# Whole expert matrices in one load each, a second pair of early input weights, first output tiles of 128 tokens, and a new order

## The chip, the cores and the metric

The kernel runs on one core of one Trainium2 chip. The metric is the time of one execution on the device in microseconds. The kernel before takes 282.68 us, the median of 3 runs (282.34 to 283.34).

## The reference

Three stages follow one another. An attention layer with 2 batches, 8 heads, 768 tokens and 64 numbers per head looks at a window of 15 tokens to each side and at 24 pooled keys. A soft mixture of 8 experts with 4 slots each sends all 1536 tokens (512 numbers each) through `phi`. A softplus layer of 2048 hidden units ends it.

```python
k_sum = k.reshape(B, H, nb, 32, D).max(axis=3); v_sum = v.reshape(B, H, nb, 32, D).mean(axis=3)
mask_l = np.abs(pos[:, None] - pos[None, :]) < 16
scores_s = scale * np.einsum('bhsd,bhnd->bhsn', q, k_sum) + np.log(32)
...                                   # softmax over [local, pooled], times [v, v_sum] -> x
logits = x @ phi
d = softmax(logits, axis=0); slot_input = (d.T @ x).reshape(8, 4, 512)
for e in range(8):
    slot_out[e] = np.maximum(slot_input[e] @ w1[e], 0.0) @ w2[e]
x = softmax(logits, axis=1) @ slot_out.reshape(32, 512)
h = x @ w_in
return (np.maximum(h, 0.0) + np.log1p(np.exp(-np.abs(h)))) @ w_out
```

The softmaxes are written out in the reference with their maximum and sum. Weights: `w1` is 8 x 512 x 1024, `w2` 8 x 1024 x 512, `w_in` 512 x 2048, `w_out` 2048 x 512, all float32 in the result. The kernel reads `w_in` and `w_out` as 64-bit numbers and cuts float32 values out of their bits.

## The kernel before, in words

Everything that the kernel issues is a task with a name and one to three numbers. Two tables, `ORDER_A` (attention, routing, loads of most expert weights) and `ORDER_B` (experts and output stage), list the tasks, and `run` calls them in that order. Each engine has its own instruction stream and takes its instructions in that order, one after the other; a suffix such as `:DVE` picks the engine of a copy. All loads and stores are issued by SP, also in that order, and SP waits when the next load's buffer isn't free. `warm n` puts n filler matmuls of 480 columns into PE's stream; their result is not used.

*Loads.* Large buffers of 128 x 4096 float32 (`slots`, s0 to s9) are used in turn for the heads' q, k and v, then for the expert matrices. Each `w1` matrix (512 rows of 4 KB, 2 MB) and each `w2` matrix (2 MB) comes in two halves of 1 MB, tasks `w1 e n` and `w2 e h`. `wi c h` loads 256 columns of the input weights (1 MB), `wo c h` 256 rows of the output weights (1 MB); the first of each come in halves of 0.5 MB (`wi 0 0 0` and `wi 0 0 1`, `wo 0 0 0` and `wo 0 0 1`).

*Conversion.* The raw 64-bit weights become float32 by one scaling on ACT (`wia`, `woa`; L720) and three integer operations on DVE (`wib c 0` to `wib c 2`, `wob`; lines L726, L728 and L731), where c now counts the loads of 256. Output weights are also split into a high part `wh` (ACT) and a low part `wl` (DVE, L779).

*Attention and routing.* Per 128 tokens and head group: scores `sc`, maximum `mx`, subtraction `sub`, exponential `ex`, transposes `tr` with copies `tc`, the product `av` and a division `dv`. Then logits (`xt`, `xc`, `lt`, `lc`, `lm`, `ln`), the softmax over tokens, and the slot inputs `siT`. Three filler matmuls stand before the second transpose of the maximum (`warm 3`).

*Experts.* For pairs of experts E, `hu E n` multiplies the slot inputs with half of each of two `w1` matrices (L801, 16 matmuls of 512 columns each), `hr` is the relu, `ht` and `hc` turn the hidden units, and `dn e h` multiplies them with half a `w2` matrix (4 matmuls), all summed in one PSUM bank. Twelve filler matmuls stand among these. The last half, expert 7's second, is apart: `so` (ACT) copies the sum, `yl` multiplies, `ya` (DVE) adds, `yt` (PE) turns it, and `ye` copies it to `soT`. `ct` and `cc` turn the combine weights.

*Output stage.* It doesn't form x: the experts' sum is first multiplied with the input weights. For the first 128 columns this is `swc 0 j` (PE, 8 matmuls), `swd` (ACT or DVE copy of the high part) and `swe` (DVE subtraction, low part), later `qa` to `qe` for four blocks at a time. The result, `SW`, is one operand of `ha n`, the hidden units of one block J of 128 hidden units for 768 tokens (two matmuls of 384 columns, L966). `hx` (ACT softplus, L974), `hh` (ACT, high part) and `hl` (DVE, low part, L779) follow, and `m n t p` adds the products with the output weights to one of six PSUM tiles of 128 tokens (L996). There are 32 visits n: J = 0 and 1 for the first 768 tokens, then J = 0 to 15 for the second 768, then J = 2 to 15 for the first; `leave` parks or adds the sums and `out` stores them. `f` has one PSUM buffer of two banks, `e` two buffers, `gh` and `gl` three each.

## Time and profile before

| | |
|---|---|
| median of 3 runs | 282.68 us (282.34 to 283.34) |
| profiled execution | 281.86 us, its span 280.1 us |
| busy: PE, PEld | 268.9 us (96%), 190.1 us (68%) |
| busy: DVE, ACT, POOL | 158.7 us (57%), 143.3 us (51%), 35.6 us (13%) |
| read from memory, written | 60.15 MB, 3.15 MB |

The engines are PE (matmul), PEld (its weight loads, which overlap it), DVE (vector), ACT (activation), POOL and SP (which issues the DMAs). Times are microseconds from the start of the span, durations of one instruction nanoseconds. A row of a table by stage has the stretch, its length, then the busy time and the number of instructions of PE, PEld, DVE, ACT and POOL, the granted clock of PE (1.00 is full), the share of the 16 DMA engines that was busy, and GB/s. A row of the chain of waits or of a timeline has the start, the duration and the instruction, out<-in by the program's names. A row of instructions by line has the count, the busy time and the mean of one in ns, then the idle time of the engine just before them and what ended it. A row of DMAs has their count, the KB of each and the us from issue to landing.

### The profile page before, as it was taken

How to read it: one execution, taken by the hardware profiler on the slowest of the kernel's cores; microseconds unless marked ns; L12 is line 12 of the kernel's file. 1: busy time of each engine (PE TensorE's matmuls, PEld its weight loads, DVE VectorE, ACT ScalarE, POOL GpSimd, SP SyncE). 2: the span in 40 equal slices, each digit the busy share in tenths (PEclk: the TensorE clock that was granted, in tenths of full speed). 3: DMA queues.
4: the chain of work that ended last, by engine and by line, in shares of the span. 5: the costliest groups of instructions: out<-in, count | busy, mean ns of one | idle time of the engine just before them, and what ended most of it. 6: DMA issues, size and time to landing. Idle time of an engine off the chain costs nothing.

```text
span 280.1 us, 5571 instructions
## 1 busy us (share of the span) xinstructions
PE 268.9 (96%) x2335; PEld 190.1 (68%) x2335; DVE 158.7 (57%) x244; ACT 143.3 (51%) x216; POOL 35.6 (13%) x91
## 2 busy tenths in 40 slices
...
GB/s 258 405 396 383 415 413 401 419 416 418 415 414 375 420 410 416 407 397 398 397 251 400 8 0 0 2 0 0 2 0 114 111 2 0 0 0 2 0 74 151
DMA packets 17064, 63.65 MB, mean 227 GB/s; under 512 B 1936, under 2 KB 2320, under 8 KB 12944
## 3 DMA queue, kind: packets, MB, share of 16 engines
...
q8 instruction: 18, 0.29, 0.4%
q14 instruction: 6, 0.05, 0.0%
HBM read 60.15 MB, written 3.15 MB: 226 GB/s over the span
## 4 chain that ended last, share of the span: by engine, by line
PE 72%; DVE 12%; ACT 6%; issue 4%; DMA 3%; SPq 1%; POOL 1%; DVEq 0%; ACTq 0%; POOLq 0%
PE acc L996 36%; PE h_ps L801 5%; PE so_ps L823 5%; PE av L365 4%; PE tpa L349 4%; PE f_ps L966 3%; DMA s<-in_k 3%; PE sc L327 2%; DVE gl L779 2%; DVE wo L728 2%; DVE wo L731 2%; ACT AB L167 2%; PE tpx L387 2%; DVE wf L728 1%; DVE whl L779 1%
## 5 line engine op out<-in xcount | busy, mean ns | idle before, releaser
L996 PE MATMUL acc<-whl,gh 128*128 128x512 f32 (+1 forms) x386 | 104.3, 392 | 0.0
L996 PEld LDWEIGHTS acc<-whl,gh 128*128 128x128 f32 x386 | 71.4, 188 | 14.3 <-issue 0.8
L779 DVE TENSOR_TENSOR gl<-e,gh 128x768 fp32r<-128x768 f32 (+1 forms) x33 | 30.3, 931 | 52.8 <-PE acc L996 26.3
L996 PE MATMUL acc<-whl,gl 128*128 128x512 f32 (+1 forms) x193 | 57.7, 393 | 0.3 <-DVE gl L779 0.3
L974 ACT ACTIVATE e<-f_ps 128x768 f32<-128x768 f32 (+1 forms) x33 | 26.0, 792 | 40.3 <-PE f_ps L966 25.0
L996 PEld LDWEIGHTS acc<-whl,gl 128*128 128x128 f32 x193 | 36.0, 188 | 9.3 <-DVE gl L779 2.0
L167 ACT ACTIVATE gh<-e 128x768 fp32r<-128x768 f32 (+1 forms) x33 | 26.7, 823 | 13.2 <-PE acc L996 12.9
L167 ACT ACTIVATE s<-s 64x520 f32<-64x520 f32 (+4 forms) x20 | 14.1, 719 | 8.3 <-DMA s<-in_v 8.0
L966 PE MATMUL f_ps<-cs 128*128 128x384 f32 x64 | 16.7, 343 | 1.1 <-ACT e L974 1.0
L365 PE MATMUL av<-s,AB 120*64 120x65 f32 x384 | 15.7, 226 | 1.0 <-ACT AB L167 0.4
L365 PEld LDWEIGHTS av<-s,AB 120*64 120x64 f32 x384 | 13.0, 137 | 5.0 <-issue 3.6
L332 DVE TENSOR_REDUCE m<-sc 128x8 f32<-128x960 f32 x12 | 13.8, 1149 | 4.2 <-PE sc L327 4.2
L167 ACT ACTIVATE AB<-tpa 120x512 f32<-120x512 f32 x23 | 13.5, 595 | 5.3 <-PE tpa L349 5.0
L259 POOL COPY s<-vs 24x520 f32<-24x520 f32 x24 | 14.2, 622 | 12.2 <-ACT vs L167 11.7
L349 PE MATMUL tpa<-ident,AB 128*120 128x128 f32 x96 | 15.0, 283 | 0.3 <-ACT vs L167 0.3
L339 DVE TENSOR_TENSOR AB<-sc,m 128x960 f32<-128x960 f32 x12 | 13.8, 1150 | 1.7 <-PE tpa L349 1.6
L966 PEld LDWEIGHTS f_ps<-cs 128*128 128x128 f32 x64 | 11.7, 188 | 4.5 <-ACT e L974 1.3
L801 PE MATMUL h_ps<-s,siT 128*32 128x512 f32 x128 | 14.4, 594 | 0.4 <-DVE siT L259 0.4
L344 ACT ACTIVATE AB<-AB 128x480 f32<-128x480 f32 x24 | 14.1, 599 | 0.3
L349 PEld LDWEIGHTS tpa<-ident,AB 128*120 128x120 f32 x96 | 10.0, 137 | 3.8 <-issue 1.3
L823 PE MATMUL so_ps<-s,hT 128*32 128x512 f32 x104 | 12.6, 599 | 0.0
L259 POOL COPY s<-s 128x384 f32<-128x384 f32 x24 | 12.1, 504 | 3.4 <-DMA s<-in_k 3.0
...
## 6 DMA issues: line engine op xcount, KB each, us to landing
s<-in_moe_w SPq DMA_DIRECT2D x30, 1024.0 KB, 12.0
wi_raw<-in_moe_w_in SPq DMA_DIRECT2D x7, 1024.0 KB, 11.4
wo_raw<-in_moe_w_out SPq DMA_DIRECT2D x7, 1024.0 KB, 15.3
...
out<-ot SPq DMA_DIRECT2D x11, 256.0 KB, 2.1
AB<-in_moe_w SPq DMA_DIRECT2D x2, 1024.0 KB, 11.9
```

Of the source, the lines that this page charges most:

```text
L167: nc.scalar.activation(out=o, in_=i, func=ACTF.Copy)
L259: (nc.vector if eng == "DVE" else nc.gpsimd).tensor_copy(out=o, in_=i)
L332: nc.vector.tensor_reduce(out=m.rearrange("p (e u) -> p e u", e=2), in_=sc_t[i][:, :, 0:480].rearrange("p e (u j) -> p e u j", u=4), axis= ...
L344: nc.scalar.activation(out=A_t[i][:, e], in_=A_t[i][:, e], func=ACTF.Exp, scale=0.125)
L349: nc.tensor.transpose(tp[0:120, u], A_t[i][:, e, u, :], ident)
L365: mm(out=av_t[i][64 * w:64 * w + 64, e, 65 * u:65 * u + 65], lhsT=AT_t[i][0:120, e, c:c + 64], rhs=v_t[g][0:120, w, 2 * n + t, 2 * a + e, ...
L779: (nc.vector if eng == "DVE" else nc.gpsimd).tensor_tensor(out=o, in0=i, in1=h.bitcast(F32), op=ALU.subtract)
L801: mm(out=h_ps[E][32 * j:32 * j + 32], lhsT=siT[:, kk], rhs=w1_t[2 * E + j // 2, n][:, kk % 2, 512 * (j % 2):512 * (j % 2) + 512], start=(k ...
L823: mm(out=so_ps[32 * m:32 * m + 32, 0], lhsT=hT[e // 4][:, e % 4, h, m], rhs=w2_t[e, h, m], start=(e == 0 and h == 0), stop=(e == 7 and h = ...
L966: mm(out=f[n][:, h, 0:384], lhsT=cs_t["SW"][:, J], rhs=cs_t["cS"][:, s0:s0 + 384], **one)
L974: nc.scalar.activation(out=e_[n][:, half(hs)], in_=f[n][:, half(hs), 0:384], func=ACTF.Softplus)
L996: mm(out=acc[(n > 1) + (n > 17), t][:, d], lhsT=g, rhs=(wh, wl, wh)[p][J][:, d], start=(n in OPEN and p == 0), stop=(n in SHUT and p == 2) ...
```

## The change

- The loads of all eight `w1` matrices and of `w2` 0 to 6 become one load of 2 MB each (`w1 e 2`, `w2 e 2`); `w2 7` keeps its halves. k and v of head groups 1 and 2 are joined as well.
- A `w2` matrix that comes whole has its rows laid over the partitions in another way: partition p holds rows 8p to 8p+7 instead of 4p to 4p+3 of each half. So that the hidden units stand in the same order, the up-projection of experts 0 to 6 reads its weights in groups of four numbers with gaps of four (`units`).
- `wi 0 1`, the second 256 input columns, is loaded behind `w2 7 1`, the last expert half, and ahead of `wo 0 0 1`; `wo 0 0 0` goes ahead of `w2 7 1`.
- The first visit's activation, copy and low part are cut into tiles of 128 tokens and the second half: `(0 0)`, `(0 1)`, `(0 2)`, `(1)`, where they were two halves of 384. `swc 0 j` is cut into two pairs of matmuls.
- The division `dv` multiplies one tile of tokens per instruction instead of one parity of heads; the instruction count stays two.
- Both order tables are new. `warm 3` is gone from `ORDER_A`; the last addition and store of the kernel are of a whole tile (`31 3`), where they were of half a tile (`31 5 1`).

```diff
@@ -16,80 +16,80 @@
 ORDER_B = """
...
-dn 5 1, wib 0 1 1, dn 5 0, wib 1 1, warm 2, warm 2, dn 7 0, so, wib 1 2, yl 1, woa 0 0, wib 0 1 2, yl 0, ya 1, yt 1,
...
+wib 0 1 1, wob 0 0 1, wob 0 0 2, dn 7 0, so, yl 0, ya 0, yl 1, ya 1, yt 0, yt 1, wi 1 0, wib 0 1 2, wi 1 1, wh 0 0,
+ct 2, wl 0 0:DVE, cc 0, ye 0:ACT, ye 1:DVE, wia 1, swc 0 0 0, wib 1 0, swc 0 0 1, swd 0 0:ACT, swc 0 1 0, swe 0 0,
...
@@ -183,6 +183,7 @@
                 tasks[m](*([eng] if eng else []))
+    WHOLE1, WHOLE2, JOINED = (0, 1, 2, 3, 4, 5, 6, 7), (0, 1, 2, 3, 4, 5, 6), (('k', 1), ('k', 2), ('v', 1), ('v', 2))
     W1 = ("s6", "s7", "s8", "s9", "s2", "s3", "s4", "s5")
     W2 = ("s0", "s1", "", "s6", "s7", "s8", "s9", "s2")
@@ -199,10 +200,11 @@
         nc.sync.dma_start(out=q_t[g][a], in_=q[g][:, a])
     def load_k(g, a):
+        a = slice(0, 2) if a == 2 else a
         nc.sync.dma_start(out=kr_t[g][:, a], in_=k[g][:, a])
     def load_v(g, n):
-        c = slice(3 * n, 3 * n + 3)
+        c = slice(0, 6) if n == 2 else slice(3 * n, 3 * n + 3)
         nc.sync.dma_start(out=v_t[g][:, 0, c], in_=v[g][:, c])
     def load_w1(e, n, tag, at_):
@@ -210,6 +212,11 @@
         t = slots[tag][:, at_:at_ + 2048].rearrange("p (k f) -> p k f", k=2)
         nc.sync.dma_start(out=t, in_=w1[e].rearrange("(p k) f -> p k f", k=4)[:, 2 * n:2 * n + 2])
         w1_t[e, n] = t
+    def load_w1_all(e, tag):
+        t = slots[tag].rearrange("p (k f) -> p k f", k=4)
+        nc.sync.dma_start(out=t, in_=w1[e].rearrange("(p k) f -> p k f", k=4))
+        w1_t[e, 0], w1_t[e, 1] = t[:, 0:2], t[:, 2:4]
     def load_w2(e, h, t, m=0):
@@ -218,6 +225,21 @@
         nc.sync.dma_start(out=t, in_=w2[e, 512 * h:512 * h + 512].rearrange("(p m) d -> p m d", m=4)[:, m:m + n])
         for j in range(n):
             w2_t[e, h, m + j] = t[:, j]
+    def load_w2_all(e, t):
+        t = t.rearrange("p (h m d) -> p h m d", h=2, m=4)
+        nc.sync.dma_start(out=t, in_=w2[e].rearrange("(p h m) d -> p h m d", h=2, m=4))
+        for h in range(2):
+            for m in range(4):
+                w2_t[e, h, m] = t[:, h, m]
+    def units(e, n, k, h):
+        t = w1_t[e, n][:, k]
+        if e in WHOLE2:
+            return t.rearrange("p (n h m) -> p n h m", h=2, m=4)[:, :, h]
+        return t[:, 512 * h:512 * h + 512]
     raw0 = {}
@@ -372,11 +394,11 @@
         rd = ap2.tile([128, 2, 4, 1], F32, tag="rd", name="rd")
         nc.vector.tensor_scalar(out=rd, in0=ps[:, :, :, 64:65], scalar1=1e-9, scalar2=None, op0=ALU.add)
         nc.vector.reciprocal(out=rd, in_=rd)
-        o = x[b][:, 2 * n:2 * n + 2, 256 * hq:256 * hq + 256].rearrange("p t (a e d) -> p t a e d", a=2, e=2)
-        for e in range(2):
+        for t in range(2):
             nc.vector.tensor_tensor(
-                out=o[:, :, :, e], in0=ps[:, e, :, 0:64].rearrange("p (t a) d -> p t a d", t=2),
-                in1=rd[:, e].rearrange("p (t a) o -> p t a o", t=2).to_broadcast([128, 2, 2, 64]), op=ALU.mult)
+                out=x[b][:, 2 * n + t, 256 * hq:256 * hq + 256].rearrange("p (a e d) -> p a e d", a=2, e=2),
+                in0=ps[:, :, 2 * t:2 * t + 2, 0:64].rearrange("p e a d -> p a e d"),
+                in1=rd[:, :, 2 * t:2 * t + 2].rearrange("p e a o -> p a e o").to_broadcast([128, 2, 2, 64]), op=ALU.mult)
     xT_t, LT_t, dp = {}, {}, {}
...
@@ -799,7 +829,7 @@
         for kk in range(2 * n, 2 * n + 2):
             for j in range(4):
                 mm(out=h_ps[E][32 * j:32 * j + 32], lhsT=siT[:, kk],
-                   rhs=w1_t[2 * E + j // 2, n][:, kk % 2, 512 * (j % 2):512 * (j % 2) + 512],
+                   rhs=units(2 * E + j // 2, n, kk % 2, j % 2),
                    start=(kk == 0), stop=(kk == 3), skip_group_check=True)
     def relu(E):
...
@@ -946,10 +980,11 @@
         o, i = quad_o(c, slice(64, 128))
         less(o, i, o)
-    def sw0_c(j):
-        o = parts["0", j] = bank("sw_ps", (128, 128))
-        for kk in range(4):
-            mm(out=o, lhsT=soT[:, kk], rhs=wf_t[0][:, kk, 128 * j:128 * j + 128], start=(kk == 0), stop=(kk == 3),
+    def sw0_c(j, h):
+        if h == 0:
+            parts["0", j] = bank("sw_ps", (128, 128))
+        for kk in range(2 * h, 2 * h + 2):
+            mm(out=parts["0", j], lhsT=soT[:, kk], rhs=wf_t[0][:, kk, 128 * j:128 * j + 128], start=(kk == 0), stop=(kk == 3),
                skip_group_check=True)
     def sw0_d(j, eng):
@@ -965,23 +1000,25 @@
             s0 = 768 * R + 384 * h
             mm(out=f[n][:, h, 0:384], lhsT=cs_t["SW"][:, J], rhs=cs_t["cS"][:, s0:s0 + 384], **one)
-    def half(hs):
-        return slice(hs[0], hs[0] + 1) if hs else slice(0, 2)
+    def part(t, hs):
+        c = slice(128 * hs[1], 128 * hs[1] + 128) if len(hs) > 1 else slice(0, 384)
+        return t[:, hs[0]:hs[0] + 1, c] if hs else t[:, :, c]
     def act(n, *hs):
         if n not in e_:
             e_[n] = fp[2].tile([128, 2, 384], F32, tag="e", name="e")
-        nc.scalar.activation(out=e_[n][:, half(hs)], in_=f[n][:, half(hs), 0:384], func=ACTF.Softplus)
+        nc.scalar.activation(out=part(e_[n], hs), in_=part(f[n], hs), func=ACTF.Softplus)
     def high(n, *hs):
         if n not in gh:
             gh[n] = fp[3].tile([128, 2, 384], FR, tag="gh", name="gh")
-        copy(gh[n][:, half(hs)], e_[n][:, half(hs)])
+        copy(part(gh[n], hs), part(e_[n], hs))
     def low(n, *hs):
         if n not in gl:
             gl[n] = fp[3].tile([128, 2, 384], FR, tag="gl", name="gl")
-        less(gl[n][:, half(hs)], e_[n][:, half(hs)], gh[n][:, half(hs)])
+        less(part(gl[n], hs), part(e_[n], hs), part(gh[n], hs))
     def cols(hs):
         return slice(256 * hs[0], 256 * hs[0] + 256) if hs else slice(0, 512)
@@ -1034,12 +1071,13 @@
         for name, fn in zip(("qa", "qb", "qc", "qd", "qe"), (quad_a, quad_b, quad_c, quad_d, quad_e)):
             task((name, c), P(fn, c))
     for j in range(2):
-        for name, fn in zip(("swc", "swd", "swe"), (sw0_c, sw0_d, sw0_e)):
+        for h in range(2):
+            task(("swc", 0, j, h), P(sw0_c, j, h))
+        for name, fn in zip(("swd", "swe"), (sw0_d, sw0_e)):
             task((name, 0, j), P(fn, j))
     for n in range(32):
         task(("ha", n), P(hid, n))
-        for h in range(2) if n == 0 else (None,):
-            hs = () if h is None else (h,)
+        for hs in ((0, 0), (0, 1), (0, 2), (1,)) if n == 0 else ((),):
             task(("hx", n) + hs, P(act, n, *hs))
             task(("hh", n) + hs, P(high, n, *hs))
             task(("hl", n) + hs, P(low, n, *hs))
```

In the order tables the following pieces matter. First PE, at the end of the experts and the start of the output stage; `so_ps` is the experts' sum, `sT_ps` its turned form, `ct_ps` and `cw` the combine weights, `sw_ps` the product with the first input weights, `f_ps` the hidden units. Before:

```order
L823 MATMUL so_ps<-s,hT_1350 32x512 x4
L834 MATMUL so_ps<-s,hT_1350 32x256 x8
L844 MATMUL sT_ps<-e_99,so 128x128 x4
L952 MATMUL sw_ps<-wf,soT 128x128 x8
L966 MATMUL f_ps<-cs 128x384 x4
L996 MATMUL acc<-whl,gh 128x512 x2
```

After:

```order
L853 MATMUL so_ps<-s,hT_1332 32x512 x16
L864 MATMUL so_ps<-s,hT_1332 32x256 x8
L874 MATMUL sT_ps<-e_99,so 128x128 x4
L740 MATMUL ct_ps<-ident,cw 128x128 x4
L987 MATMUL sw_ps<-wf,soT 128x128 x8
L1001 MATMUL f_ps<-cs 128x384 x2
L1033 MATMUL acc<-whl,gh 128x512 x2
```

The last block of combine weights (`ct 2`) moved behind the turning of the sum, and only one visit's hidden units, not two, stand ahead of the first output matmuls.

Second DVE, from the sum of the experts to the subtraction that the first visit needs; `wf` are converted input weights, `wo` converted output weights, `whl` their low part, `cs` holds `SW`. Before:

```order
L838 TENSOR_TENSOR so<-so_ps,so 128x256 x2
L726 TENSOR_SCALAR wo<-wo 128x512
L728 SCALAR_TENSOR_TENSOR wo<-wo_raw,wo 128x512
L259 COPY soT<-sT_ps 128x256
L731 SCALAR_TENSOR_TENSOR wo<-wo_raw,wo 128x512
L726 TENSOR_SCALAR wo<-wo 128x512
L779 TENSOR_TENSOR cs<-sw_ps,cs 64x128
```

After:

```order
L868 TENSOR_TENSOR so<-so_ps,so 128x256 x2
L761 SCALAR_TENSOR_TENSOR wf<-raw_1369,wf 128x2x256
L809 TENSOR_TENSOR whl<-wo,whl 128x512
L281 COPY soT<-sT_ps 128x256
L756 TENSOR_SCALAR wf<-wf 128x4x256
L809 TENSOR_TENSOR cs<-sw_ps,cs 64x128
```

Ahead of the copy to `soT` stand a conversion of input weights and the first low part of output weights instead of two conversions of output weights; behind it one conversion instead of two.

Third SP's queue of loads at the end of the expert weights; `s` are expert matrices (2048 numbers per partition are half a matrix, 4096 a whole one), `wi_raw` and `wo_raw` raw input and output weights. Before:

```order
L218 DMA s<-in_moe_w 128x2048 x7
L236 DMA wi_raw<-in_moe_w_in 128x4x512
L218 DMA s<-in_moe_w 128x2048 x3
L246 DMA wo_raw<-in_moe_w_out 128x1024 x2
L246 DMA wo_raw<-in_moe_w_out 128x2x1024 x2
```

After:

```order
L225 DMA s<-in_moe_w 128x2048
L232 DMA s<-in_moe_w 128x4096 x4
L268 DMA wo_raw<-in_moe_w_out 128x1024
L225 DMA s<-in_moe_w 128x2048
L258 DMA wi_raw<-in_moe_w_in 128x4x512
L268 DMA wo_raw<-in_moe_w_out 128x1024
```

The second pair of input weights stood three expert halves ahead of the output weights; it now stands behind the last expert half, and the first output weights stand ahead of that half.

## Rows read from the trace of the kernel before

**Rows 1.** Table by stage, five stretches of the span.

```profile
0.00:82.50 82.50, 77.69 (x1224) 53.02 (x1224) 54.43 (x106) 53.54 (x97) 35.56 (x91) 1.00 0.99 396
82.50:117.43 34.93, 34.57 (x288) 11.01 (x292) 11.49 (x28) 7.86 (x11) 0.00 (x0) 1.00 1.00 405
117.43:122.35 4.92, 4.07 (x44) 3.22 (x36) 3.46 (x9) 2.87 (x6) 0.00 (x0) 1.00 1.02 406
122.35:186.75 64.40, 63.04 (x383) 48.31 (x383) 62.27 (x71) 48.26 (x64) 0.00 (x0) 1.00 0.48 181
186.75:276.35 89.60, 89.52 (x402) 74.50 (x402) 26.29 (x30) 30.74 (x40) 0.00 (x0) 1.00 0.07 26
```

**Rows 2.** Chain of waits from 72 to 126 us: start, duration, instruction.

```profile
74.36 0.61 PE wm L661 x3
...
111.55 0.59 PE ct_ps L710 x4
...
116.62 1.04 PE so_ps L823 x8
...
117.74 0.61 ACT so L167
...
120.49 2.07 PE sw_ps L952 x16
...
123.00 0.88 ACT e L974 x2
```

**Rows 3.** Timeline of PE: the hidden units of visits 0 and 14.

```profile
122.35 0.61 PE L966 MATMUL f_ps<-cs 128*128 128x384 f32 x2
...
186.75 0.62 PE L966 MATMUL f_ps<-cs 128*128 128x384 f32 x2
```

**Rows 4.** Waits from 122 to 187 us: total us, count, longest.

```profile
PEld f_ps L966 <- DVE cs L779: 1.0, 2, 0.5
```

**Rows 5.** Timeline of SP: issue of `w2 7 1` and of `wo 0 0 0`.

```profile
96.54 1.89 SPq L218 DMA_DIRECT2D s<-in_moe_w  x1
...
99.09 1.82 SPq L246 DMA_DIRECT2D wo_raw<-in_moe_w_out  x1
```

**Rows 6.** Landing of the same two loads.

```profile
s<-in_moe_w SPq DMA_DIRECT2D x1, 1024.0 KB, 20.2
...
wo_raw<-in_moe_w_out SPq DMA_DIRECT2D x1, 512.0 KB, 19.5
```

**Rows 7.** Instructions by line and shape: durations that the sum uses.

```profile
L801 PE MATMUL h_ps<-s,siT 128*32 128x512 f32 x128 | 14.4, 594 | 0.4 <-DVE siT L259 0.4
...
L731 DVE SCALAR_TENSOR_TENSOR wf<-raw,wf 128x512 int32<-128x512 int32 x2 | 1.4, 690 | 0.0
L779 DVE TENSOR_TENSOR whl<-wo,whl 128x512 fp32r<-128x512 f32 x2 | 1.4, 688 | 0.0
L167 ACT ACTIVATE cs<-sw_ps 128x128 fp32r<-128x128 f32 x1 | 0.3, 277 | 0.7 <-PE sw_ps L952 0.7
L720 ACT ACTIVATE wf<-wi_raw 128x1024 f32<-128x1024 f32 x7 | 8.1, 1156 | 5.7 <-DMA wi_raw<-in_moe_w_in 5.7
L779 DVE TENSOR_TENSOR cs<-sw_ps,cs 64x128 fp32r<-64x128 f32 x2 | 0.6, 294 | 0.2 <-ACT cs L167 0.2
L779 DVE TENSOR_TENSOR gl<-e,gh 128x768 fp32r<-128x768 f32 x31 | 29.2, 955 | 52.8 <-PE acc L996 26.3 <-ACT gh L167 26.3
```

**Rows 8.** Table by stage: loads with long rows, then with short ones.

```profile
60.00:75.00 15.00, 13.68 (x177) 9.52 (x175) 5.57 (x20) 8.03 (x17) 0.00 (x0) 1.00 1.01 417
120.00:140.00 20.00, 18.57 (x102) 14.25 (x102) 19.63 (x29) 16.59 (x27) 0.00 (x0) 1.00 1.03 396
```

**Rows 9.** Landing of the last stores.

```profile
out<-ot SPq DMA_DIRECT2D x3, 256.0 KB, 2.4
out<-ot SPq DMA_DIRECT2D x2, 128.0 KB, 2.0
```

**Rows 10.** Timeline of DVE: the last additions.

```profile
276.35 0.76 DVE L1010 TENSOR_TENSOR ot<-acc,park 128x256 f32<-128x256 f32 x2 [0.70 <-PE acc L996]
```

More of the change, by code (lines that the diff above doesn't have):

```diff
@@ L29 @@
-wo 2 0, wob 2 0, wob 2 1, m 1 1, leave 1 3:DVE, hh 2, hl 2, m 2 3, leave 1 4:ACT, m 2 2, wh 1, leave 1 0:ACT, wob 2 2,
-leave 1 1:DVE, wib 2 0, swa 1, m 2 1, leave 1 2:ACT, swb 1:ACT, ha 3, m 2 0, leave 1 5:DVE, wl 1:DVE, m 2 5, wi 2 0,
-m 2 4, wia 3, wib 2 1, hx 3, hh 3, wib 3 0, swc 1, swd 1:ACT, hl 3, m 3 1 0, swe 1, m 3 1 1, ha 4, wo 1 1, wib 3 1,
-wib 2 2, wib 3 2, woa 3, hx 4, m 3 2 0, m 3 0 0, hh 4, hl 4, ha 5, m 3 0 1, hx 5, wo 2 1, wh 2, m 4 1 0, hh 5, wi 2 1,
-qa 1, qb 1:ACT, wia 4, m 4 0 1, qc 1, wl 2:DVE, hl 5, wob 3 0, m 5 0 0, m 3 2 1, qd 1:ACT, qe 1, m 4 2 0, ha 6,
@@ new lines @@
+m 0 0, hh 0 0 2, hl 0 0 2, wob 0 1 2, hx 0 0 1, m 0 2, hx 0 1, hh 0 1, wo 2 0, swe 0 1, hh 0 0 1, hl 0 1, m 0 3,
+m 0 5, wib 1 1, wh 0 1, hl 0 0 1, ha 1, m 0 4, woa 1, cc 2, hx 1, m 0 1, wl 0 1:DVE, hh 1, ha 2, wib 1 2, hl 1, swa 1,
+m 1 0, m 1 3, wia 2, wob 1 0, wi 2 0, m 1 1, leave 1 0:ACT, wob 1 1, m 1 4, hx 2, m 1 2, m 1 5, hh 2, wob 1 2, hl 2,
+m 2 5, leave 1 4:ACT, swb 1:ACT, m 2 2, leave 1 3:DVE, ha 3, wia 3, leave 1 2:ACT, m 2 3, wib 2 0, wib 3 0, hx 3,
+leave 1 1:DVE, m 2 1, m 2 0, swc 1, wh 1, leave 1 5:DVE, hh 3, wo 2 1, wi 2 1, swd 1:ACT, wib 3 1, m 2 4, wl 1:DVE,
@@ new lines @@
+swe 1, hl 3, wo 1 1, m 3 1 0, ha 4, m 3 0 0, m 3 0 1, wia 4, hx 4, wib 2 1, wib 3 2, ha 5, woa 2, hh 4, wib 2 2, hx 5,
+wob 2 0, m 3 2 0, m 3 1 1, wob 2 1, hh 5, wia 5, m 4 1 1, qa 1, qb 1:ACT, m 4 0 0, wib 4 0, qc 1, wi 3 0, hl 5,
+wob 2 2, m 5 0 1, m 3 2 1, qd 1:ACT, woa 3, qe 1, wib 4 1, wo 3 1, m 5 2 1, ha 6, m 5 1 1, m 5 2 0, m 4 0 1, hx 6,
+wh 2, hl 4, m 5 1 0, ha 7, m 4 2 0, hh 6, hx 7, wib 4 2, m 5 0 0, ha 8, wob 3 0, m 4 1 0, wib 5 0, hl 6, wo 3 0, hh 7,
+m 4 2 1, wl 2:DVE, m 7 0 0, hx 8, m 6 0 0, hl 7, ha 9, m 6 1 0, wib 5 1, hx 9, woa 5, wi 3 1, wob 3 1, wib 5 2, hh 9,
@@ new lines @@
+m 7 2 0, wia 6, qa 2, m 7 2 1, m 7 0 1, qb 2:ACT, wob 3 2, wob 5 0, m 6 0 1, wh 3, qc 2, m 6 1 1, m 6 2 1, m 6 2 0,
+wob 5 1, wl 3:DVE, m 7 1 0, qd 2:ACT, wia 7, hl 9, qe 2, woa 4, m 9 2 1, m 7 1 1, ha 10, hh 8, wob 5 2, wob 4 0,
+wib 7 0, m 8 1 0, wh 5, m 8 0 0, hx 10, hh 10, m 9 1 1, ha 11, m 8 0 1, m 9 0 1, hl 8, hx 11, wob 4 1, ha 12, m 8 2 0,
+hl 10, wib 6 0, wl 5:DVE, m 8 2 1, wob 4 2, wib 6 1, m 9 2 0, hx 12, m 8 1 1, wh 4, m 9 1 0, ha 13, hh 12, wib 7 1,
+m 9 0 0, woa 6, m 10 2 1, m 10 0 1, hh 11, m 12 0 1, wl 4:DVE, m 12 1 1, wib 7 2, hl 12, hx 13, wib 6 2, m 12 2 0,
@@ L89 @@
[L89 to L92 removed]
+k 0 0, km 0 0, kf 0 0 1:Pool, k 0 1, warm 28, q 0 0, bias, q 0 1, kf 0 0 2:Pool, kf 0 0 0:Pool, v 0 0, v 0 1, k 1 2,
```

139 lines of the change are left out of this document (69 added, 70 removed).

## The prediction

> **What bounds the kernel now.** I read the table by stage first, then the chain of waits, then the waits of the last stage, then the loads, then the durations.
>
> The table by stage [rows 1] cuts the span where the work changes: attention and routing (0 to 82.5 us), the experts (82.5 to 117.43), a turn from the experts to the output stage (117.43 to 122.35), the output stage while weights are still being converted (122.35 to 186.75), and the rest of it. The reader is to see that PE is busy 34.57 of 34.93 us among the experts, 63.04 of 64.40 in the fourth stretch and 89.52 of 89.60 in the fifth, and that DVE is busy 62.27 of 64.40 in the fourth. So the fifth stretch is PE's and can't shrink: whatever its start gains, the end gains. The fourth is shared: PE waits there for what DVE makes, and one such wait stands just before its end, when `ha 14` (the hidden units of visit 14, at 186.75 us [rows 3]) needs the last quad of combined weights. PE waited twice, 1.0 us in all, for such quads [rows 4].
>
> The chain of waits [rows 2] runs on PE alone through the experts up to 117.66 us (the end of `dn 7 0`, 116.62 + 1.04), then ACT copies the sum of the experts (117.74), DVE adds the last expert's half, PE turns it and multiplies it with the first input weights (120.49), and ACT starts the first activation at 123.00.
>
> The loads run beside this. The half matrix `w2 7 1` was issued at 96.54 and took 20.2 us [rows 5, 6], so it landed at 116.7, just before PE wanted it; the first half of output weights was issued at 99.09, took 19.5 and landed at 118.6.
>
> **The sum, step by step.** It is made against the profiled execution's own 281.86 us (span 280.1 and 1.76 around it). The median of the runs shown is 282.68, 0.82 more, so I carry the difference over to 282.68.
>
> *Loads.* Up to and with `wi 0 1` the new queue sends the same bytes as the old one up to and with `wo 0 0 0`: the two have changed places. So `wi 0 1` lands where `wo 0 0 0` did, at 118.6; `w2 7 1` is ahead of it by 1 MB, which at the 396 GB/s of small-row loads [rows 8] is 2.6 us: 116.0. Joining halves leaves the bytes alone. Its price I bound by the two rates of rows 8: loads with rows of 2 KB ran at 396 GB/s, loads with rows of 8 KB at 417, 5% more for rows four times as long. For rows twice as long again I allow 0 to 5% on the 31.5 MB that come whole, 0 to 3.6 us, and take 0 for the sum, because these loads already keep all 16 engines full (share 1.01).
>
> *Routing.* The three filler matmuls before the second transpose go. They stand in the chain for 0.61 us [rows 2], which is the most they can give back; 0 is the least, if what follows them waits for the vector engine's maximum anyway. I take 0.4, nearer the row. The rest of attention is a new order of the same instructions. PE idles 82.5 − 77.69 = 4.8 us there [rows 1]; that bounds the gain, and I take as much for a loss. I put 0 in the sum, since ACT and DVE are busy 54 us each of the same stretch and nothing in the trace says which waits the new order meets.
>
> *Experts.* The same 128 up-projection records, the same down projections, the same 12 fillers. One block of four transposes, `ct 2`, 0.59 us [rows 2], moves from before `dn 7 0` to a place where PE waits anyway, behind the last sum's transposes. By rate, PE reaches the end of `dn 7 0` at 117.66 − 0.59 − 0.4 = 116.7. `w2 6` whole lands ahead of `wo 0 0 0` and `w2 7 1`, 1.57 MB, so 1.57 MB / 417 GB/s = 3.8 us before 116.0, at 112.2, and `w2 7 1` at 116.0, both before PE asks, so I cost the joining at 0 here; the cover is thin (0.7 us), and a load later than that is paid one for one. Up-projections now read groups of four numbers with gaps of four. No row before reads that way. The nearest are these same matmuls without gaps, 594 ns [rows 7]; I take no change, and for the range I keep both a gain of nothing and a doubling.
>
> *The turn.* From the end of `dn 7 0` to the copy 0.08, copy 0.6, two additions, as before. Then DVE has two conversions ahead of its copy of `soT`: `wib 0 1 2` at 690 and `wl 0 0` at 688 ns [rows 7], 1.3 us with the overlap of starts. Counted from 116.7: copy done 117.4, additions done 118.2, conversions 119.5, `soT` 119.9, the second half of J=0's matmuls (a quarter of the 2.07 us of rows 2) 120.45, ACT copy 277 ns 120.75, subtraction 294 ns 121.1, `ha 0` at 121.15. Before it was 122.35: a gain of 1.2 us. `wia 1` on ACT (1156 ns) begins at 118.8, after `wi 0 1` has landed; that is hidden by DVE's conversions.
>
> *First tiles.* The first activation takes 128 columns instead of 384. The two halves took 0.88 us [rows 2], so one of 384 is 0.44; I estimate 0.28 for 128 from the 277 ns copy of that size. Activation, copy and the second tile's activation together bring the first product 0.3 to 0.5 us nearer to `ha 0`. It is worth only what the next step leaves.
>
> *DVE in the fourth stretch.* From the subtraction before `ha 0` to `ha 14` both orders give PE 71 groups of output matmuls and 14 visits. DVE's list differs by little: three small `hl 0 0 x`, `wob 0 1 0` and two conversions of `wib 1` come in, `hl 0 0`, `wl 0 0` and two conversions of `wob 6` leave, 0.05 us net. But `hl 12` (955 ns [rows 7]) now stands before the last quad's subtraction instead of behind it: +0.95. DVE's idle time there was 64.40 − 62.27 = 2.1 us [rows 1]; the new order puts other work between a conversion and the subtraction that waits for ACT, so some of it goes. The bounds are 0 and 2.1; I take 0.8. So `ha 14` moves by −1.2 + 0.95 − 0.8 = −1.05, to 185.7.
>
> *End.* The fifth stretch is the same work. The last store is now a whole tile, landing in 2.4 us where the half tile took 2.0 [rows 9]; the last addition was in two halves of 256, 0.76 together [rows 10], of which only the second, 0.38, came after the last matmul, and is now one of 512, about 0.7 by the 688 ns of that width [rows 7]. I take +0.25 for both, between 0 and 0.7.
>
> Sum: −1.05 + 0.25 = −0.8, so 281.06 for a profiled execution, and 281.9 against the median. I say 281.8, since the one cost I set to 0 with a bound on one side only (joined loads) can only help.
>
> **A rule weighed.** Rows 8 show 1 MB loads following each other at 417 GB/s. The Trainium skill (DMA: Bandwidth & Descriptors, Measured) has a table in which 1 MB reaches 341 GB/s and 16 MB 425. By that, one load of 2 MB beats two of 1 MB. The trace does not agree for loads in a queue: 417 at 1 MB leaves almost nothing to win. By the rule the sum would be up to 3 us lower where loads decide.
>
> The doubtful step is the read with gaps. The Trainium skill (SBUF — State Buffer, Door 1: The DMA port swizzle, its note on cachelines) says that reads which hit the same 16-byte line at least twice go at full speed. Four numbers of four bytes fill a line, so by it the gaps are free; no run here shows it.
>
> **Rivals.**
> 1. *DVE takes it all* (0.25). If DVE's idle 2.1 us stays, `ha 14` moves by −1.2 + 0.95 = −0.25 and the end takes that back: 282.7. For it: the waits of rows 4, and DVE's 97% in that stretch. Against it: the longest single idle is a wait for a copy that the new order covers.
> 2. *More than I count* (0.2). Attention loses some of its 4.8 us of PE idle, or whole loads run faster. `wi 0 1` at 118.6 then becomes the gate: 1.16 + 0.6 + 0.29 behind it put `ha 0` at 120.75 at the earliest with today's rate. With 0.4 more there and all of DVE's idle gone, −1.6 + 0.95 − 2.1 + 0.25 = −2.5: 280.2.
> 3. *Slower: whole matrices wait for whole slots* (0.14). `w2 3` may start only when three up-projection blocks are done, the old half after one less; SP is in order, so everything behind waits, `wi 0 1` last. ACT takes `wia 1` before the copy that `ha 0` needs, and DVE `wib 1 0` before its subtraction, so a late `wi 0 1` stops both. It decides from 120.2 us on (118.6 + 1.6), where `ha 0` is at 122.35 again. Three us of gaps in the stream give `ha 0` at 123.75, +1.4, and with DVE's +0.95, −0.8 and the end's 0.25: 284.5.
> 4. *Slower: the read with gaps or the new order of attention costs PE time* (0.1). PE is the bound through both. Seven of eight up-projection matrices are read so; 10% on 14.4 us is 1.25 us and brings back 283, a doubling is 12.5 us and 294. Attention worse by 3 us gives 284.9.
>
> **How the numbers follow.** The forecast has 0.31 and its own range 280.9 to 282.4. A change of under 0.3% (0.85 us) can't be told from none here. Faster than 281.83 are all of rival 2 and most of the forecast's range (0.28): 0.48. Within 0.3% are the rest of the forecast and nearly all of rival 1: 0.28. Slower are rivals 3 and 4: 0.24. The range 279.6 to 284.8 leaves out about 1 in 10 above (the doubling, long gaps) and less than 1 in 10 below.
>
> **What would show it.** In the changed kernel: `wi 0 1` lands near 118.6; no wait of PE for a load among the experts above 0.5 us; the up-projection still at 594 ns; `ha 0` near 121.15; the last quad's subtraction ends near 185.6 with DVE's idle time before it under 1.5 us; from `ha 14` to the last output matmul 89.6 us. I am wrong if `ha 0` comes after 122.35, if the up-projection's mean rises, or if PE's idle time in the fourth stretch grows by as much as the start gains.

## The result, and the profile after

The changed kernel takes 280.35 us, the median of 4 runs (279.43 to 280.87), against 283.01 (282.34 to 284.34) for the kernel before: ratio 0.9897, interval 0.9848 to 0.9946. In a second session it took 280.60 (8 runs, 279.26 to 281.59) against 283.37 (17 runs, 281.86 to 285.79): 0.9903, 0.9864 to 0.9942. It is faster by about 1%, 2.7 us, where 0.9 us was forecast.

The profiled execution took 279.86 us, with a span of 278.1. That is 2.0 us below the profiled execution of before, and this difference can be followed row by row. The table by stage of the changed kernel, cut at the same events as [rows 1] (copy of `siT`, start of the last half's matmuls, `ha 0`, `ha 14`, end of the last output matmul):

```profile
0.00:81.31 81.31, 74.92 (x1221) 52.08 (x1221) 54.72 (x106) 53.34 (x97) 35.55 (x91) 1.00 0.99 401
81.31:115.51 34.20, 33.85 (x285) 10.63 (x288) 9.72 (x27) 6.84 (x10) 0.00 (x0) 1.00 1.00 403
115.51:120.65 5.14, 4.71 (x48) 3.62 (x40) 3.38 (x8) 3.87 (x7) 0.00 (x0) 1.00 1.01 389
120.65:185.22 64.57, 62.93 (x381) 48.60 (x382) 63.49 (x74) 47.77 (x66) 0.00 (x0) 1.00 0.49 186
185.22:274.36 89.14, 89.14 (x403) 74.33 (x401) 27.40 (x32) 32.25 (x41) 0.00 (x0) 1.00 0.07 26
```

The lengths of the stretches are to be compared, not their shares: attention and routing are 1.2 us shorter, the experts 0.7, the turn is 0.2 longer, the stretch with conversions 0.2 longer, the last stretch 0.4 shorter. For a finer cut, and to see what repeats, the same events were read from every profile of this study. All times are us; "first max" is the start of DVE's first maximum of scores, "copy" ACT's copy of the experts' sum, "last" the end of the last output matmul; the last column ends with the span, which is given to 0.1 us:

| kernel | first max at | to `siT` | to copy | to `ha 0` | to `ha 14` | to last | to the end |
|---|---|---|---|---|---|---|---|
| before | 10.28 | 72.23 | 35.23 | 4.61 | 64.40 | 89.57 | 3.78 |
| before_again | 10.12 | 72.24 | 35.23 | 4.93 | 64.43 | 89.58 | 3.87 |
| changed | 10.06 | 71.25 | 34.51 | 4.83 | 64.57 | 89.14 | 3.74 |
| after_again | 10.28 | 71.52 | 34.51 | 4.82 | 64.62 | 89.13 | 3.82 |
| oldA_newB | 11.12 | 71.90 | 34.51 | 4.84 | 64.59 | 89.13 | 3.81 |
| newA_oldB | 10.71 | 71.78 | 35.23 | 4.61 | 64.47 | 89.53 | 3.87 |
| halves | 11.23 | 71.53 | 34.51 | 4.82 | 64.60 | 89.12 | 3.79 |
| warm3 | 10.30 | 71.64 | 34.51 | 4.83 | 64.59 | 89.12 | 3.81 |
| wib10_late | 9.64 | 71.25 | 34.51 | 4.61 | 65.07 | 89.13 | 3.79 |
| wi01_early | 11.08 | 71.81 | 35.33 | 4.98 | 64.60 | 89.14 | 3.76 |
| first_halves | 9.94 | 71.53 | 34.51 | 4.83 | 65.08 | 89.14 | 3.77 |
| every_second | 10.98 | 71.25 | 35.32 | 4.82 | 64.59 | 89.15 | 3.79 |
| fill24 | 10.23 | 71.60 | 34.51 | 4.82 | 64.58 | 89.13 | 3.83 |
| fill20 | 9.51 | 72.07 | 34.50 | 4.83 | 64.60 | 89.12 | 3.77 |

Behind `siT` the columns repeat to about 0.05 us wherever an order is kept, but for one wait in before_again (told below), so differences of 0.1 us are real there although the whole time scatters by over 2 us. The scatter sits in the first two columns, and it isn't the change's: kernels with the same attention start their first maximum anywhere from 9.64 to 11.23.

The turn, from ACT's copy to `ha 0`, in the timeline of the changed kernel (start, duration, instruction, idle time before it):

```profile
115.82 0.60 ACT L167 ACTIVATE so<-so_ps 128x512 f32<-128x512 f32 x1 [3.17 <-PE so_ps L853]
...
118.40 1.15 ACT L750 ACTIVATE wf<-wi_raw 128x1024 f32<-128x1024 f32 x1
...
119.58 0.69 DVE L756 TENSOR_SCALAR wf<-wf 128x1024 int32<-128x1024 int32 x1 [0.62 <-ACT wf L750]
119.77 0.28 ACT L167 ACTIVATE cs<-sw_ps 128x128 fp32r<-128x128 f32 x1 [0.22 <-PE sw_ps L987]
...
120.31 0.29 DVE L809 TENSOR_TENSOR cs<-sw_ps,cs 64x128 fp32r<-64x128 f32 x1
...
120.65 0.62 PE L1001 MATMUL f_ps<-cs 128*128 128x384 f32 x2
```

DVE begins a conversion at 119.58, as soon as ACT has made its input, and the subtraction that `ha 0` needs stands behind it: ACT's copy ends at 120.05, the subtraction starts at 120.31.

The loads of the changed kernel (KB, us from issue to landing), `w2 7 1` issued at 100.95 and, in the second group, `wi 0 1` issued at 101.43:

```profile
s<-in_moe_w SPq DMA_DIRECT2D x1, 1024.0 KB, 13.0
...
wi_raw<-in_moe_w_in SPq DMA_DIRECT2D x1, 1024.0 KB, 15.4
```

`w2 7 1` lands at 113.95, 1.56 us before PE starts on it at 115.51. Before, it landed at 116.7 [rows 5, 6], 0.7 before PE.

### The profile page after: what moved, and what is told of

Read it like the earlier page. It is cut to its first block, busy times and chain, and to the rows that moved or that the text cites. A ratio compares the mean times of both kernels' runs of the same rounds, so it can differ in the third digit from the quotient of the medians.

```text
span 278.1 us, 5546 instructions
## 1 busy us (share of the span) xinstructions
PE 265.6 (95%) x2332; PEld 189.3 (68%) x2332; DVE 159.4 (57%) x246; ACT 144.1 (52%) x220; POOL 35.5 (13%) x91
## 4 chain that ended last, share of the span: by engine, by line
PE 74%; DVE 11%; ACT 11%; issue 2%; ACTq 0%; DVEq 0%
PE acc L1033 37%; PE h_ps L831 5%; PE so_ps L853 5%; PE tpa L371 3%; PE f_ps L1001 3%; PE av L387 3%; PE wm L691 3%; ACT s L167 3%; ACT AB L366 2%; PE sc L349 2%; DVE wf L758 2%; ACT AB L167 2%; PE tpx L409 2%; DVE whl L809 2%; DVE gl L809 1%
## 5 line engine op out<-in xcount | busy, mean ns | idle before, releaser
L809 DVE TENSOR_TENSOR gl<-e,gh 128x768 fp32r<-128x768 f32 (+2 forms) x35 | 30.9, 886 | 56.5 <-ACT gh L167 38.8
L1011 ACT ACTIVATE e<-f_ps 128x768 f32<-128x768 f32 (+2 forms) x35 | 26.3, 756 | 31.6 <-PE f_ps L1001 26.2
L167 ACT ACTIVATE gh<-e 128x768 fp32r<-128x768 f32 (+2 forms) x35 | 27.3, 789 | 26.2 <-PE acc L1033 25.9
L387 PE MATMUL av<-s,AB 120*64 120x65 f32 x384 | 14.1, 225 | 0.4 <-DVE x L398 0.4
L387 PEld LDWEIGHTS av<-s,AB 120*64 120x64 f32 x384 | 12.3, 137 | 3.0 <-issue 2.2
L750 ACT ACTIVATE wo<-wo_raw 128x1024 f32<-128x1024 f32 (+1 forms) x9 | 9.4, 1042 | 9.5 <-DMA wo_raw<-in_moe_w_out 9.5
```

The source lines that it names most:

```text
L167: nc.scalar.activation(out=o, in_=i, func=ACTF.Copy)
L387: mm(out=av_t[i][64 * w:64 * w + 64, e, 65 * u:65 * u + 65], lhsT=AT_t[i][0:120, e, c:c + 64], rhs=v_t[g][0:120, w, 2 * n + t, 2 * a + e, ...
L809: (nc.vector if eng == "DVE" else nc.gpsimd).tensor_tensor(out=o, in0=i, in1=h.bitcast(F32), op=ALU.subtract)
L1011: nc.scalar.activation(out=part(e_[n], hs), in_=part(f[n], hs), func=ACTF.Softplus)
```

## The experiments

**The two order tables apart.** oldA_newB has `ORDER_A` of before (with its halves), newA_oldB `ORDER_B` of before:

```diff
-WHOLE1, WHOLE2, JOINED = (0, 1, 2, 3, 4, 5, 6, 7), (0, 1, 2, 3, 4, 5, 6), (('k', 1), ('k', 2), ('v', 1), ('v', 2))
+WHOLE1, WHOLE2, JOINED = (), (3, 4, 5, 6), ()                    # oldA_newB, with ORDER_A of before
+WHOLE1, WHOLE2, JOINED = (0, ..., 7), (0, 1, 2), (('k', 1), ...)  # newA_oldB, with ORDER_B of before
```

> The changed kernel with the attention and routing order of before (its loads in halves, `warm 3` in it), and the new order for experts and output stage. Theory 1 (the new order of attention gives 1.2 us, the new order of the rest the other 0.8): `siT` is copied at 82.5 us again, the distance from there to `ha 0` stays 39.3 us as in the changed kernel (40.2 before), and the span is 279.3. Rival (the joined loads set attention's end): the same `siT`, but the weights land about 2 us later than in the changed kernel, PE waits for `w2 7 1` or `wi 0 1`, and `ha 0` comes at 122.3 or later: span 280. Rival (the gain in attention comes from the division by token tile, which this kernel keeps): `siT` at 81.3 and span 278.

> The changed kernel with the order of before for experts and output stage (`wi 0 1` ahead of the last expert halves, expert matrices 3 to 7 in halves, first visit in two halves), and the new attention. Theory 1: `siT` at 81.3, `ha 0` 1.2 us earlier than before (121.15), span 278.9, because the old order's distances stay as they were. Rival (DVE takes it all, as in the prediction's first rival): `ha 0` at 121.15, but `ha 14` at 186.5 and span 279.8. Rival (loads): the expert halves still land at the old times (`w2 7 1` at 116.7), PE waits 1.2 us for it at the last half, and the span is 280.

Measured: oldA_newB 281.81 us (10 runs), ratio 0.9958 (0.9926 to 0.9990); newA_oldB 281.58 (10 runs), 0.9954 (0.9921 to 0.9988). Each half of the change is faster by itself, and within the scatter the two gains add up. Nor did PE wait for loads in either: their columns behind `siT` are those of the kernel whose `ORDER_B` they have. The table gives the parts: the new `ORDER_B` brings 35.23 to 34.51, 4.61 to 4.84, 64.40 to 64.59 and 89.57 to 89.13 in whichever kernel it stands, −0.74 together. In attention one has to take pauses out first (more on them in the last section). Before took 72.23 from the first maximum to `siT`; one set of 32 score matmuls took 1.31 us at 32.67, where others took 0.99:

```profile
29.30 0.99 PE L327 MATMUL sc<-s 64*64 64x120 f32 x32
...
32.67 1.31 PE L327 MATMUL sc<-s 64*64 64x120 f32 x32
```

before_again has such a pause at another place (1.30 at 10.08) and the same 72.24. oldA_newB, the same order with the new division, has none, and takes 71.90: the division is worth nothing, the pause 0.33. With the new order every profile has a longer pause, always in the same set: the 32 matmuls took 1.42 in the changed kernel, and from profile to profile `siT` moves with their length one for one. Without pauses, then, the old order takes 71.9 and the new one 71.25 − 0.43 = 70.8. The first rival of newA_oldB's expectation, DVE taking it all, did not come: its `ha 0` to `ha 14` stayed at 64.47.

**Whole loads.** halves sends each joined load as its two halves, one after the other:

```diff
-... w2 4 2, ... w1 7 2, ... k 1 2, ...
+... w2 4 0, w2 4 1, ... w1 7 0, w1 7 1, ... k 1 0, k 1 1, ...   (and WHOLE1, WHOLE2, JOINED empty)
```

> The changed kernel with every joined load cut into its two halves again at the same place of the order (and the up-projection's reads without gaps again). Theory 1 (joining gives bandwidth only, and the order already covers it): the loads up to `wi 0 1` land about 1.8 us later (118.6 instead of 116.8), `w2 7 1` at 115.8 just behind the moment PE wants it (115.5), so the span grows by 0.3 to 0.5 us to 278.5; `siT` stays at 81.3; up-projection 594 ns as before. Rival (joining earns the gain of attention): `siT` at 82.3 and span 279.2. Rival (joining costs slot waits): span 277.7, faster than the changed kernel.

Measured: 280.73 us (6 runs), ratio 0.9907 (0.9880 to 0.9934), within the scatter of the changed kernel. Every column behind `siT` is the changed kernel's, and counted from `siT`, `wi 0 1` landed at 35.6 us against 35.5. Joining the loads gives no time and takes none; neither the bandwidth that theory 1 granted it nor the slot waits of the rival show in the time. Nor does it earn attention's gain: 71.53 with halves, and after_again, whose loads are joined, has 71.52.

The experiment also gives the price of the gaps in the up-projection's reads, since without joined loads they are read without gaps; every_second asks for wider ones:

```diff
-return t.rearrange("p (n h m) -> p n h m", h=2, m=4)[:, :, h]
+return t.rearrange("p (n h) -> p n h", h=2)[:, :, h]
```

> The changed kernel with the up-projection of experts 0 to 6 reading every second number instead of groups of four with gaps of four (the hidden units then stand in another order than the rows of `w2`, so the output is not the reference's). Theory (a matmul's moving operand is read at the pace of its columns whatever the gaps in this range): 595 ns and 16.7 us of up-projections, as in the changed kernel. Rival (groups of four are what makes the gaps free): over 700 ns, and the experts longer by 2 us or more.

Measured: its one execution took 281.62 us. Instructions by line (count, busy us, mean ns), first of halves, then of every_second:

```profile
L831 PE MATMUL h_ps<-s,siT 128*32 128x512 f32 x128 | 14.6, 595 | 0.4 <-DVE siT L281 0.4
```

```profile
L831 PE MATMUL h_ps<-s,siT 128*32 128x512 f32 x128 | 15.4, 615 | 0.4 <-DVE siT L281 0.4
```

The changed kernel's matmuls also take 595 ns: groups of four with gaps of four cost nothing. Every second number costs 20 ns a matmul and 0.81 us in the experts' column (35.32), so neither theory was quite right: gaps are not free in general, and the price is far from a doubling. The Trainium skill (Advanced Engine Details and Errata, Memory Cachelines) says that at least two hits on a 16-byte line are needed to absorb the access latency. The groups of four (four hits) ran at full pace, which agrees; every second number (two hits) meets this too and still took 3% longer here.

**The fillers of the routing.** warm3 puts them back:

```diff
-zt 1, dm, zl 0, da, zx 1:DVE, ...
+zt 1, dm, zl 0, da, warm 3, zx 1:DVE, ...
```

> The changed kernel with the three filler matmuls back ahead of the routing's next transpose, at the place they had. Theory (they stood in the chain): `siT` at 81.9 (0.6 later) and span 278.7. Rival (the maximum's broadcast waits for DVE anyway): `siT` at 81.3 to 81.4, span 278.1. Second rival (the clock falls without them, or rises with them): the granted clock before 82 us differs; it was 1.00 in both kernels.

Measured: 280.49 us (7 runs), ratio 0.9912 (0.9881 to 0.9942). `siT` comes 71.64 us behind the first maximum; two kernels without the fillers have 71.52 and 71.53 with the same pause in the scores, so the fillers cost 0.1 us, not 0.6. They stood in the chain of before [rows 2], and do so again in warm3 with the same 0.61 us; but in their absence the chain has DVE's work in that place (0.30 and 0.24 us, and a transpose behind it). The granted clock was 1.00 there with the fillers as without them, so the second rival is out.

**The conversion ahead of the first subtraction.** wib10_late:

```diff
-swc 0 0 0, wib 1 0, swc 0 0 1, swd 0 0:ACT, swc 0 1 0, swe 0 0, swc 0 1 1,
+swc 0 0 0, swc 0 0 1, swd 0 0:ACT, swc 0 1 0, swe 0 0, wib 1 0, swc 0 1 1,
```

> The changed kernel with one conversion (`wib 1 0`, 0.69 us on DVE, which waits for ACT's `wia 1`) moved from ahead of the first subtraction to behind it. Theory (DVE holds the subtraction that `ha 0` waits for, 120.31 instead of 120.05): `ha 0` at 120.4 instead of 120.65, `ha 14` the same amount earlier or not at all, span 277.8 to 278.1. Rival (PE is bound by its own matmuls there): `ha 0` at 120.65, span 278.1.

Measured: 280.46 us (4 runs), ratio 0.9888 (0.9849 to 0.9927), no different from the changed kernel. `ha 0` came 4.61 us behind the copy instead of 4.83, as the theory said: the conversion is what made the turn longer. But `ha 0` to `ha 14` grew from 64.57 to 65.07. So the 0.22 was given back twice over; its expectation of "the same amount earlier or not at all" missed that. Waits of PE's weight loads for DVE's low parts from `ha 0` to `ha 14` (total us, count, longest), first in wib10_late, then in the changed kernel:

```profile
PEld acc L1033 <- DVE gl L809: 1.5, 4, 0.5
```

```profile
PEld acc L1033 <- DVE gl L809: 0.8, 3, 0.4
```

**The place of `wi 0 1`.** wi01_early:

```diff
-hc 2 1, w2 5 2, ...   ... ct 1, wi 0 1, ct 0, ...
+hc 2 1, wi 0 1, w2 5 2, ...   ... ct 1, ct 0, ...
```

> The changed kernel with `wi 0 1` sent ahead of `w2 5`, where it stood before, and nothing else moved. Theory (the place of this 1 MB in the queue decides whether the last expert half is there in time): `w2 7 1` lands 2.5 us later, at 116.4 instead of 113.95, PE waits 0.9 us for it where it now wants it (115.5), `ha 0` at 121.5, span 278.9 or, where DVE's stretch gives the wait back, 278.4. Rival (transfer hidden either way): no wait, span 278.1.

Measured: 281.71 us (7 runs), ratio 0.9938 (0.9908 to 0.9968). `w2 7 1` landed at 102.52 + 15.6 = 118.1, and PE waited. Its landing, and PE's waits for loads from 100 to 120 us in this kernel (total us, count, longest):

```profile
s<-in_moe_w SPq DMA_DIRECT2D x1, 1024.0 KB, 15.6
```

```profile
PE so_ps L853 <- DMA s<-in_moe_w: 0.8, 1, 0.8
```

The columns to the copy and to `ha 0` grow by 0.82 and 0.15, and the next one gives none of it back. So the place of 1 MB in the queue is worth 1.0 us of this kernel (2.6 us of transfer less the 1.56 us by which `w2 7 1` was early), and it is the one part of the change tried here whose worth the loads decide.

**The first tiles.** first_halves:

```diff
-        c = slice(128 * hs[1], 128 * hs[1] + 128) if len(hs) > 1 else slice(0, 384)
+        c = slice(0, 384)      # and the tasks (0 1) and (0 2) do nothing
```

> The changed kernel with the first visit's activation, copy and low part in two halves of 384 columns again. Theory (the tiles of 128 bring the first product 0.3 to 0.5 us nearer to `ha 0` and DVE's chain behind it takes that back): first product 1.75 us behind `ha 0` instead of 1.39, `ha 14` at 185.2 to 185.4, span 278.1 to 278.3. Rival (the tiles are worth their time to the end): `ha 14` at 185.6, span 278.5.

Measured: 281.03 us (9 runs), ratio 0.9932 (0.9901 to 0.9962). Timeline of PE in this kernel, then in the changed one, at the first output product:

```profile
120.81 0.62 PE L1001 MATMUL f_ps<-cs 128*128 128x384 f32 x2
122.63 0.73 PE L1033 MATMUL acc<-whl,gh 128*128 128x512 f32 x2 [1.20 <-ACT gh L167]
```

```profile
122.04 0.73 PE L1033 MATMUL acc<-whl,gh 128*128 128x512 f32 x2 [0.77 <-ACT gh L167]
```

PE idles 1.20 us for the first operand instead of 0.77, and `ha 0` to `ha 14` is 65.08 instead of 64.57: the rival holds, the tiles are worth their 0.43 us to the end and a little more.

**Both kernels once more, and the start.** after_again and before_again are the two kernels unchanged; fill24 and fill20 have fewer fillers ahead of the first scores:

```diff
-k 0 1, warm 28, q 0 0,
+k 0 1, warm 24, q 0 0,      # fill24; warm 20 in fill20
```

> The changed kernel once more, for a second profile and a closer ratio. In the profiles so far all that comes behind the copy of `siT` repeats within 0.05 us for one order, and the time of that copy differs by up to 2 us between kernels with the same attention, by when the 28 fillers at the start end (8.4 to 10.0 us) and by one pause in the scores (0.4 to 1.0 us). Theory (only the start and that pause vary): `siT` to `ha 14` 103.9, `ha 14` to the last output matmul 89.1, the rest of the span by the start; ratio to before 0.992 to 0.995, since 1.4 to 1.7 us of the first profile's 2.0 belong to the change. Rival (the change gives 2.6 us, the profile of before was a lucky one): ratio 0.989 to 0.991.

> The kernel before once more, for a second profile. Theory (its profile of the start of this study is an ordinary one): first maximum to `siT` 71.9 to 72.3, the stages behind it as they were (34.92, 4.92, 64.40, 89.57). Rival (it pauses more often than the changed kernel, and the first profile missed that): first maximum to `siT` 72.8 or more, or later stages longer by over 0.3.

> The changed kernel with 24 instead of 28 filler matmuls ahead of the first scores. Theory (the first scores wait for the fillers, which run at 0.12 us each by then): first scores 0.4 to 0.9 us earlier, `siT` by as much, the time 0.4 to 0.9 us below the changed kernel. Rival (the operands are made by POOL until 8.6 us, so the first scores can't come earlier): `siT` unchanged. Second rival (with fewer fillers PE comes to its full pace later): same or slower.

> The changed kernel with 20 instead of 28 filler matmuls ahead of the first scores. Theory (fillers gate the first scores until POOL's copies do): the fillers end between 7.3 and 8.5 us, the first scores come at 7.4 to 8.6, and the time falls by 0.5 to 1.4 us against the changed kernel; if POOL's copies gate, all runs start their scores at the same time and the spread shrinks. Rival: PE, waiting for the copies, runs the first scores at its slower pace and `siT` comes later than with 24.

Measured: after_again 280.60 us (8 runs), ratio as above; before_again's one execution 282.08; fill24 280.11 (6 runs, 279.12 to 281.52), 0.9897 (0.9857 to 0.9937); fill20 280.32 (11 runs, 279.01 to 282.26), 0.9907 (0.9879 to 0.9935).

after_again repeats the changed kernel's columns, but its ratio is the rival's; what goes with that stands under *Open* below. before_again repeats before's except the one to `ha 0`, which is 0.32 longer. Its waits between 81 and 126 us, and a row of its chain of waits, name the cause:

```profile
PEld so_ps L834 <- DMA s<-in_moe_w: 1.0, 1, 1.0
```

```profile
97.32 20.15 DMA s<-in_moe_w
```

`so_ps` L834 are the last half's matmuls. `w2 7 1` landed at 97.32 + 20.15 = 117.47 here, 0.7 us later than in the first profile, while PE was ready 0.15 us earlier, and PE waited for it. The kernel before has no room for such a load; in the changed one 1.56 us lie between.

The fillers don't decide the start alone. They stand 0.20 us apart by then, not the 0.12 of fill24's theory. With 24, PE was ready at 8.47 and then waited for a load of q; with 20 the first maximum came at 9.51, and a longer pause in the scores (1.09 us between two matmuls) took it back. No version tried here is clearly faster than the changed kernel.

## Why the prediction was right in its direction, and short

The range held the time and the sign was right. The forecast of −0.8 for a profiled execution met −2.0, and the median moved by −2.7. Step by step, in us:

| step of the prediction | forecast | profile | what the runs showed |
|---|---|---|---|
| start of the first scores | 0 | −0.22 | scatter of the start |
| routing and attention | −0.4 | −0.98 | −0.1 the fillers, −1.0 the rest of the new order, +0.1 by pauses (0.43 instead of 0.33) |
| experts: `ct 2` moved | −0.59 | −0.72 | the same with the new `ORDER_B` in either kernel; `ct 2` was not moved by itself |
| turn | −0.2 | +0.22 | the conversion `wib 1 0` ahead of the subtraction |
| stretch with conversions | +0.15 | +0.17 | −0.5 of the first tiles in it |
| last stretch | 0 | −0.44 | two waits for DVE are gone |
| end | +0.25 | −0.04 | no cost of the last whole tile |

*Attention.* The term set to 0, the new order, is what was mis-sized: it measured −1.0. The prediction bounded it by 4.8 us of PE idle both ways and had no row to choose by, and the bound itself was on the wrong quantity. In the changed kernel PE idles 81.31 − 74.92 = 6.4 us of this stretch, 1.6 more than before, while its busy time fell by 2.8. Some 0.8 of that are the three fillers; 1.6 are the `av` matmuls, the same 384 with the same mean. Rows by line, before and after:

```profile
L365 PE MATMUL av<-s,AB 120*64 120x65 f32 x384 | 15.7, 226 | 1.0 <-ACT AB L167 0.4
```

```profile
L387 PE MATMUL av<-s,AB 120*64 120x65 f32 x384 | 14.1, 225 | 0.4 <-DVE x L398 0.4
```

In the timelines they stand in eleven runs of 32 in a row (1.15 us each) and two of 16 (0.69), where there were six and twelve. That this is what shortens the stretch is not shown: no kernel changed it alone. The prediction gave the whole routing gain to the three fillers. They were on the chain and yet worth 0.1: a row in the chain says that something ends last, not that nothing else ends just before.

*Turn.* DVE's list of work ahead of `soT` was read well: the copy to `soT` was there at 118.54, before PE wanted it. The step that failed is "that is hidden by DVE's conversions": `wia 1` on ACT ended only at 119.55, DVE waited 0.62 us for it, and then did the conversion ahead of the subtraction. (The earliest `ha 0` of the second rival, 120.75, is 0.1 more than its terms add up to. `ha 0` came at 120.65, but `wi 0 1` had landed 1.8 us before the time that this rival starts from.)

*Stretch with conversions.* The sum came out, by another way than forecast. DVE's idle time fell from 2.1 to 64.57 − 63.49 = 1.1 us [rows 1], as the prediction took it. But the last quad is no longer what `ha 14` waits for: its subtraction starts at 183.80 and takes 0.70, `ha 14` starts at 185.22:

```profile
183.80 0.70 DVE L809 TENSOR_TENSOR cs<-q_ps,cs 64x512 fp32r<-64x512 f32 x1
```

```profile
185.22 0.51 PE L1001 MATMUL f_ps<-cs 128*128 128x384 f32 x2
```

So that +0.95 − 0.8 meets the measured +0.17 is in part luck. And the first tiles, which the prediction counted only as far as a next step leaves them something, carry 0.5 us through the whole stretch; without them the stretch would have been 0.7 longer than before.

*Last stretch.* "So the fifth stretch is PE's and can't shrink" is the step that failed most plainly. PE was busy for 89.52 of 89.60 us [rows 1], yet it got 0.44 shorter with the same matmuls. Timelines of PE's weight loads, of PE and of DVE in the kernel before, late in that stretch:

```profile
265.34 0.41 PEld L996 LDWEIGHTS acc<-whl,gh 128*128 128x128 f32 x2
266.22 0.19 PEld L996 LDWEIGHTS acc<-whl,gl 128*128 128x128 f32 x1 [0.47 <-DVE gl L779]
```

```profile
265.56 0.61 PE L996 MATMUL acc<-whl,gh 128*128 128x512 f32 x2
266.22 0.50 PE L996 MATMUL acc<-whl,gl 128*128 128x512 f32 x1
266.56 0.63 PE L996 MATMUL acc<-whl,gh 128*128 128x512 f32 x2
```

```profile
265.21 1.83 DVE L779 TENSOR_TENSOR gl<-e,gh 128x768 fp32r<-128x768 f32 x2 [2.50 <-ACT gh L167]
```

A product with a low part waits there for DVE, which makes two of them in a row, 1.83 us from 265.21. Their neighbours start 0.23 us apart; spaced like them, the three matmuls from 265.56 to 266.56 would take 0.68 us instead of 1.00. So 0.32 us is lost here, and 0.12 at `ha 14`, whose weights waited for the last quad. The new order has neither. Matmul ends are modelled, so the busy share hid this wait, and the row of waits showed it.

*Loads.* `wi 0 1` landed at 116.8, not 118.6. Joining is not the reason (halves); counted from `siT` the same bytes landed after 35.5 us instead of 36.1, and the rest is the earlier `siT`. The third rival, slot waits, had its mechanism: SP stood from 92 to 100.57 before it could send the next load. With halves it stood as well, from 93.9 to 102.01, and came free at the same distance from `siT` (19.3 us), so the wait isn't the joining's. It cost nothing, since all landed in time.

*The second rival.* Its 280.2 is the recorded time nearest to the 280.35 measured, but not by its mechanism: PE's idle time in attention rose, and DVE kept half of its 2.1 us.

*Open.* The two profiles of before (281.86 and 282.08) and the two of the changed kernel (279.86 and 280.37) differ by 1.9 us on average, the medians by 2.7 to 2.8. The granted clock, averaged over each execution, goes with the rest. Of the 17 runs of before in the second session 10 had 0.992 to 0.994, and took 283.23 to 285.79 us; of the 8 of the changed kernel one had (281.59). All others had 0.997 or more, and among them the medians are 282.42 (7 runs) and 280.37 (7 runs): 2.05 us apart, as the profiles are. Chosen in the same way, the runs beside oldA_newB and newA_oldB have 282.42 for before, 281.64 and 281.41. So about 2.0 us of the difference is there at equal clock, and the other 0.7 comes with the low means: 33 of 56 runs of before have one, and 1 of 12 of the changed kernel. A mean of 0.993 over 283 us lacks 2.0 us of full clock (an estimate from these numbers), and by the medians those runs of before are 1.2 to 1.9 us longer. Every profiled execution has 0.997 or more, so where in the kernel the clock was low, what PE did just before, and why the new order meets it so rarely stays open, and that it is the cause is not shown.
